# Second linear layer of a Winograd MLP with its matmul operands exchanged: tokens loaded as weights, weight columns streamed

## The chip, the cores and the metric

The kernel runs on one core of a Trainium2 chip. TensorE multiplies: it loads one operand (up to 128 x 128) and streams columns of the other past it into PSUM, which has eight banks of 128 x 512 floats. VectorE, ScalarE and GpSimd work element by element, SyncE issues most of the transfers, and 16 DMA engines carry them out. The metric is the device time of one execution in microseconds. Three runs of the kernel before took 874.29, 878.18 and 880.20 us.

## What is computed

Attention in which the heads are mixed before and after the softmax, then two linear layers with a SiLU between them:

```python
scores = einsum('bhij,hg->bgij', scale * q @ k.T, w_pre)      # 4 x 12 heads x 448 x 448
attn   = einsum('bhij,hg->bgij', softmax(scores), w_post)
x      = (attn @ v) laid out as 1792 tokens x 768
h      = x @ w_in                                             # w_in 768 x 2048
g      = h * (1 / (1 + exp(-h)))
out    = g @ w_out                                            # w_out 2048 x 768, float32
```

The change touches the last line alone.

## The kernel before

The first 440 us are attention. Both linear layers then use one level of a Winograd scheme with seven products: the tokens fall into two halves (u = 0, 1 count blocks of 448 tokens in a half), the inner dimension and the outer dimension into two halves each, and each product (k or m, 0 to 6) multiplies a sum or difference of token blocks by a sum or difference of weight blocks. The weight combinations are made on the fly from float64 input by `convert` (L38 to L100) during attention and the first layer and stored in DRAM (`wi_dram`, `wo_dram`), and come back through SyncE's queue as parts `wl` (L602).

Float32 accuracy is kept by halves: an operand x is cast to a rounded `high` part on ScalarE (`wh`, L607; `halve`, L626), and the rest is a subtraction (GpSimd for weights, L608; VectorE for tokens, L628). A product is then three matmuls per block: high x high, high x low, low x high.

The second layer of before has steps ("o", m, u, a), with a one of the three blocks of 128 output features (HC = 3) and HF = 8 blocks of the inner dimension. `product` (L611) makes one step: 24 matmuls, weights of 128 x 128 loaded and 448 token columns streamed, into one PSUM bank `ph`; four banks rotate. So the result has features on partitions. `evacuate` (L791) adds the products up on VectorE and ScalarE: U, V and the results. `put_out` (L835) turns each of the 24 results of 128 features x 448 tokens by four TensorE transposes into `ptt` (L842), copies them with the scale by ScalarE (L843) and stores them in rows of 128 features (L844).

The order of everything is written out by hand: a loop over the steps (L849) emits for each step its product, then the casts of weights due (`high_at`), the loads due (`load_at`), the transposes and stores of a finished result, the evacuation of the step before, and the pieces of `begin[s]`, where `put_at` (L638) has spread the token halves for the next product and the Winograd differences (`subtract`, L632). Engines wait for each other by semaphores alone, so each engine's own order is what this loop has emitted for it.

Of the kernel before, what the change touches and what calls it, by code (L numbers as in the profile page):

```python
# [103 lines left out]
def talking_heads_then_silu_mlp(  # L104
# [348 lines left out]
    jobs += [(wo_src[:, c, f], wo_dram[:, c * HF + f]) for c in range(HC) for f in range(HF)]  # L453
# [118 lines left out]
    box, gr = {}, {}  # L572
# [3 lines left out]
    steps = [(kind, k, u, a) for kind, n in (("i", HF), ("o", HC)) for k in range(7) for u in range(NU) for a in range(n)]  # L576
    step_of = {x: s for s, x in enumerate(steps)}
    NP = HF * HC // 4
    parts = [(src, ORDER[k], p) for src in (wi_dram, wo_dram) for k in range(7) for p in range(NP)]

    def part_of(kind, k, n):
        return ((kind == "o") * 7 + k) * NP + n // 4
# [3 lines left out]
    load_at, high_at = [[] for _ in steps], [[] for _ in steps]  # L586
    for j in range(WB, len(parts)):
        kind, m = ("i", "o")[j // (7 * NP)], j // NP % 7
        kind0, m0, p0 = ("i", "o")[(j - WB) // (7 * NP)], (j - WB) // NP % 7, (j - WB) % NP
        n = HC if kind0 == "i" else HF  # L590
        s = step_of[kind0, m0, NU - 1, (4 * p0 + 3) // n] + 1
        s = max(s, step_of[kind, m, 0, 0] - (10 if kind == "i" or m == 0 else 3))
        load_at[s].append(j)
        high_at[s + (2 if s < step_of["o", 0, 0, 0] - 2 else 1)].append(j)

    def load_part(j):
        src, k, p = parts[j]
        if src is wo_dram:
            for _ in conv:
                pass  # L600
        raws[j] = box["w"].tile([128, 4, 128], F32R, name="wl", tag="wl", bufs=WB)
        nc.sync.dma_start(out=raw(raws[j]), in_=src[:, 4 * p:4 * p + 4, k])  # L602

    def ready_part(j):
        wl = raws.pop(j)
        wh = box["w"].tile([128, 4, 128], F32R, name="wh", tag="wh", bufs=WB)
        nc.scalar.copy(out=wh, in_=raw(wl))  # L607
        nc.gpsimd.tensor_sub(out=wl, in0=raw(wl), in1=raw(wh))  # L608
        ready[j] = wh, wl

    def product(s, p):  # L611

        kind, k, u, a = steps[s]
        nk = HC if kind == "i" else HF
# [9 lines left out]
    def halve(src, dst):  # L624

        nc.scalar.copy(out=dst[:, 0], in_=src)  # L626
        yield
        nc.vector.tensor_sub(out=dst[:, 1], in0=src, in1=raw(dst[:, 0]))  # L628
# [16 lines left out]
    for kind, n, nk, blocks in (("i", HF, HC, xs), ("o", HC, HF, gr)):  # L645
        for m in range(7):
            for u in range(NU):
                s = step_of[kind, m, u, 0]
                todo = [lambda b=blocks, c=c, u=u, at=SOURCE[m]: halve(b[u][(*at, c)], ops[u][c]) for c in range(nk)]
                if m or u:  # L650
                    put_at(s - n, n - (kind == "i"), todo)
                elif kind == "o":
                    put_at(s - HF, HF - 1, todo)
        for d, (x, y, z) in enumerate(DIFFER):
            for u in range(NU):
                s = step_of[kind, d, u, 0] if kind == "o" or d > 1 else step_of[kind, 0, u, 0]
                put_at(s, n - 1 if kind == "i" else n, [
                    lambda b=blocks, c=c, u=u, x=x, y=y, z=z: subtract(
                        nc.vector, b[u][(*x, c)], b[u][(*y, c)], b[u][(*z, c)]) for c in range(nk)])
# [116 lines left out]
    ops[1] = [pair(gw, f"op1{c}") for c in range(HC)]  # L776
    for u in range(NU):
        gr[u] = {}
        for i, l in ((0, 1), (0, 0), (1, 1), (1, 0)):
            for f in range(HF):  # L780
                if (i, l) == (1, 0) and f < HC:
                    gr[u][i, l, f] = xs[u][0, 1, f]
                else:
                    gr[u][i, l, f] = gw.tile([128, T], F32, name=f"g{u}{i}{l}{f}")
    ps_t = pool("ps_tt", 3, space=PSUM)
    outs, sums, spare = [], [], []
# [4 lines left out]
    def evacuate(s, p):  # L791

        kind, k, u, a = steps[s]
        p = p[:, :T]
        if kind == "i":
            U, V = gr[u][1, 1, a], gr[u][0, 1, a]
        else:
            U, V = xs[u][0, 0, a], vp[a][:, u]
        M = firsts[:, a] if (kind, u) == ("i", 0) and k in (1, 3) and a < len(phs) else U

        def target(i, l):
            if kind == "i":
                return gr[u][i, l, a]
            return box["o"].tile([128, T], F32, name="oT", tag="oT", bufs=2)

        def finish(t, i, l, sign):
            if kind == "i":
                silu(t, sign)
            else:
                outs.append(lambda: put_out(2 * u + l, HC * i + a, t, sign))  # L810

        if k == 0:
            nc.scalar.copy(out=U, in_=p)
        elif k == 1:
            t = target(0, 0)
            nc.vector.tensor_add(out=t, in0=p, in1=M)
            finish(t, 0, 0, -1.0)
# [7 lines left out]
        elif k == 5:  # L825
            t = target(1, 0)
            nc.vector.tensor_sub(out=t, in0=U, in1=p)
            finish(t, 1, 0, 1.0)
        else:
            for (i, l), x in (((1, 1), U), ((0, 1), V)):  # L830
                t = target(i, l)
                nc.vector.tensor_add(out=t, in0=p, in1=x)  # L832
                finish(t, i, l, 1.0)

    def put_out(b, c, oT, sign):  # L835
        pt = ps_t.tile([128, 512], F32, name="ptt", tag="ptt")
        if spare:
# [56 lines left out]
    while outs:  # L894
        outs.pop(0)()
# [29 lines left out]
```

## Time and profile before

| | us |
|---|---|
| median of three runs (lowest, highest) | 878.18 (874.29, 880.20) |
| the profiled execution: time, span | 879.6, 877.9 |
| TensorE, VectorE, ScalarE, GpSimd busy in the span | 832.4, 625.6, 526.6, 406.7 |
| mean granted TensorE clock | 0.976 of full speed |

The span runs from the first to the last instruction of the program. PE is the matmul part of TensorE and PEld its weight loads, which overlap with matmuls; DVE is VectorE, ACT ScalarE, POOL GpSimd, SP SyncE. A matmul's shown duration reaches to the end of its pipeline, so successive ones overlap; the time from one to the next is read from counts in a stretch. The first layer lies at about 436 to 653 us, the second at 653 to 869, and what follows is the end of the last results.

### The profile page before, as it was taken

Reading aid. Unit: us, or ns where it says so; the run is one execution under the profiler, and the core shown is the slowest. Engines: PE = TensorE matmul, PEld = TensorE weight load, DVE = VectorE, ACT = ScalarE, POOL = GpSimd, SP = SyncE. Lnnn points to the kernel's source line nnn. Section 1 sums busy time; section 2 is a strip of 40 time slices with the busy share of each in tenths; the row PEclk is TensorE's granted clock in tenths of the full one; section 3 lists DMA queues with packets and bytes.
Section 4 is the critical chain, followed back from the end, with each engine's and each line's share of the span. In section 5 each row is a group of like instructions: output and inputs, shape, how many; then the busy total and the mean of one; then the engine's idle time right before and its main releaser. Section 6 shows DMA issues by size and latency. Waiting matters only on the chain.

```text
span 877.9 us, 27521 instructions
## 1 busy us (share of the span) xinstructions
PE 832.4 (95%) x11076; PEld 661.0 (75%) x11076; DVE 625.6 (71%) x1218; ACT 526.6 (60%) x1178; POOL 406.7 (46%) x679
## 2 busy tenths in 40 slices
PE   7998999899997999799899999999999999999997
PEld 5455676566665666466699999988899989999886
DVE  5554776477865877475788899999987689984332
ACT  4676887578875887587756653325694345343242
POOL 6131545353553645274877577556741233133020
PEclk8899999799998999899999999999999999999999
DMA  8668778787788777674625543455331142112224
GB/s 168 189 171 206 204 196 231 203 223 207 221 229 221 214 203 213 167 231 153 182 100 182 161 152 114 120 152 163 95 94 49 35 114 67 40 49 72 80 77 105
DMA packets 163655, 132.89 MB, mean 151 GB/s; under 512 B 51811, under 2 KB 157263, under 8 KB 163527
## 3 DMA queue, kind: packets, MB, share of 16 engines
q1 hardware_dynamic: 161299, 129.48, 52.8%
q8 instruction: 87, 1.43, 0.7%
q10 hardware_dynamic: 1812, 0.99, 0.5%
q0 software_dynamic: 416, 0.66, 0.3%
q14 instruction: 41, 0.34, 0.1%
HBM read 64.01 MB, written 27.53 MB: 104 GB/s over the span
## 4 chain that ended last, share of the span: by engine, by line
PE 74%; DVE 9%; DMA 5%; ACT 5%; issue 3%; POOL 2%; SPq 1%; ACTq 1%; POOLq 0%; DVEq 0%
PE ph L622 40%; PE pa L437 9%; PE po L368 8%; PE pp L399 7%; PE pqk L339 7%; DMA g<-st 3%; ACT e L409 1%; DVE nm L405 1%; DVE g L822 1%; ACT at L446 1%; DVE cg L92 1%; PE ptt L842 1%; DVE op L628 1%; PE pt L269 1%; PE pt L310 1%
## 5 line engine op out<-in xcount | busy, mean ns | idle before, releaser
L622 PE MATMUL ph<-op,wh 128*128 128x448 f32 x924 | 222.8, 369 | 2.7 <-DVE g L832 1.8
L608 POOL TENSOR_TENSOR wl<-wl,wh 128x512 fp32r<-128x512 f32 x84 | 122.6, 1475 | 153.6 <-ACT wh L607 150.2
L622 PEld LDWEIGHTS ph<-op,wh 128*128 128x128 f32 x924 | 172.4, 189 | 18.9 <-DVE g L832 2.1
L405 DVE TENSOR_REDUCE nm<-pp 128x1 f32<-128x448 f32 x184 | 106.0, 618 | 81.5 <-PE pp L399 81.1
L425 POOL TENSOR_SCALAR wr<-wpost,r 128x60 f32<-128x60 f32 x184 | 72.5, 407 | 185.0 <-DVE r L422 127.9
L409 ACT ACTIVATE e<-pp,nm 128x448 f32<-128x448 f32 x184 | 115.4, 631 | 45.4 <-DVE nm L405 42.7
L437 PEld LDWEIGHTS pa<-wr,e 64*64 64x64 f32 (+1 forms) x5888 | 98.4, 133 | 45.4 <-issue 27.4
L437 PE MATMUL pa<-wr,e 64*64 64x60 f32 (+1 forms) x5888 | 110.5, 221 | 14.4 <-ACT at L446 7.3
L622 PE MATMUL ph<-op,wl 128*128 128x448 f32 x462 | 119.5, 367 | 0.0
L66 POOL TENSOR_TENSOR cg<-cw,cg 128x256 f32<-128x256 f32 x96 | 75.6, 787 | 74.0 <-DVE cw L63 70.8
L399 PE MATMUL pp<-g,wpre 64*64 64x448 f32 x736 | 102.8, 578 | 6.4 <-ACT e L409 3.4
L368 PE MATMUL po<-at,v 120*64 120x120 f32 (+1 forms) x1536 | 88.8, 269 | 6.5 <-issue 4.9
L622 PEld LDWEIGHTS ph<-op,wl 128*128 128x128 f32 x462 | 87.1, 189 | 7.5 <-POOL wl L608 0.5
L446 ACT COPY at<-pa 120x960 f32<-120x960 f32 x92 | 89.9, 977 | 4.8 <-PE pa L437 4.8
L368 PEld LDWEIGHTS po<-at,v 120*64 120x64 f32 x1536 | 78.2, 140 | 19.3 <-issue 11.2
L607 ACT CAST wh<-wl 128x512 fp32r<-128x512 f32 x84 | 51.0, 617 | 53.4 <-DMA wl<-wo_dram 26.9
L344 DVE COPY st<-pqk 120x448 f32<-120x448 f32 (+1 forms) x89 | 54.8, 617 | 33.0 <-PE pqk L339 18.1
L90 ACT ACTIVATE cg<-cg,ebias 128x256 int32<-128x256 int32 x96 | 49.5, 516 | 39.2 <-DVE cg L86 37.8
L92 DVE SCALAR_TENSOR_TENSOR cg<-cw,cg 128x256 int32<-128x256 int32 x96 | 56.0, 583 | 17.9 <-ACT cg L90 17.5
L622 PE MATMUL ph<-x,wh 128*128 128x448 f32 x252 | 64.9, 366 | 0.0
L339 PEld LDWEIGHTS pqk<-kh,qh 64*120 64x120 f32 (+1 forms) x186 | 18.9, 176 | 45.8 <-issue 15.9
L346 ACT COPY st<-pqk 120x448 f32<-120x448 f32 (+1 forms) x89 | 48.0, 539 | 6.6 <-DMA g<-st 3.4
(120 smaller groups left out, 1381.1 us busy)
## 6 DMA issues: line engine op xcount, KB each, us to landing
g<-st SPq DMA_DIRECT2D x132, 210.0 KB
cw<-in_moe_w_in SPq DMA_DIRECT2D x48, 256.0 KB
cw<-in_moe_w_out SPq DMA_DIRECT2D x48, 256.0 KB
wi_dram<-cg SPq DMA_DIRECT2D x24, 448.0 KB
wo_dram<-cg SPq DMA_DIRECT2D x24, 448.0 KB
wl<-wi_dram SPq DMA_DIRECT2D x42, 256.0 KB
wl<-wo_dram SPq DMA_DIRECT2D x42, 256.0 KB
g<-st SPq DMA_DIRECT2D x48, 175.0 KB
```

The source lines that it names most:

```text
L66: nc.gpsimd.tensor_mul(out=e, in0=m, in1=e)
L92: nc.vector.scalar_tensor_tensor(out=e, in0=hi, scalar=-2 ** 31, in1=e, op0=ALU.bitwise_and, op1=ALU.bitwise_or)
L339: nc.tensor.matmul(ps[i][:m, :S], lhsT=q_[rows, hh, :m], rhs=k_[rows], start=(step == 0), stop=(step == 2))
L368: nc.tensor.matmul(po[i * D:(i + 1) * D, c * m:(c + 1) * m], lhsT=vs[b, h][:, i, j, :], rhs=ats[n][:, j, h + i, :m], start=(j == 0), stop= ...
L399: nc.tensor.matmul((self, other)[r].p[HP * c:HP * (c + 1), :S], lhsT=wpre[rows], rhs=gs[self.n][rows, o // R + c * np + p, :], start=True, ...
L405: nc.vector.tensor_reduce(out=self.nm, in_=self.p[:GP, :S], axis=AX.X, op=ALU.max, negate=True)
L409: nc.scalar.activation(out=self.e, in_=self.p[:GP, :S], func=AF.Exp, bias=self.nm, scale=1.0, accum_out=sums)
L425: nc.gpsimd.tensor_scalar(out=g.wr, in0=wpost.rearrange("p g i -> p (g i)"), scalar1=r[:, i:i + 1], scalar2=1.0, op0=ALU.mult, op1=ALU.mult)
L437: nc.tensor.matmul(half[64 * c:64 * c + m, s, j * GH:(j + 1) * GH], lhsT=g.e[rows, j * JT + c * JH:j * JT + c * JH + m], rhs=g.wr[rows], s ...
L446: nc.scalar.copy(out=ats[self.n].rearrange("p j g t -> p (j g) t")[:, :, o:o + 2 * R].rearrange("p x (c i) -> p x c i", i=RH), in_=pa[:KV] ...
L608: nc.gpsimd.tensor_sub(out=wl, in0=raw(wl), in1=raw(wh))
L622: nc.tensor.matmul(p[:, :T], lhsT=w, rhs=x, start=(n == 0), stop=(n == len(todo) - 1))
```

## The change

In the second layer the operands change places. For a block c of 128 tokens (seven blocks in 896 tokens, over both u) the halves of the tokens are loaded as the 128 x 128 operand, and the weights of one inner block f, now 384 features wide, are streamed. A step is ("o", k, g, c): group g holds the two inner blocks f = 2g and 2g + 1, so it has six matmuls. All seven c go through group 0, then all through group 1, and so on; the seven sums of a product stay open in seven PSUM banks (four `ph`, three `pt`) until group 3. A result is then 128 tokens x 384 features, tokens on partitions, and is stored as it is.

Token tiles of the second layer are now one tile of 2 x 448 for both u, so a cast, a subtraction or a difference covers 896 columns. `outer[f]` holds the two halves of f. The half of f for product m + 1 is made when group f // 2 of product m is through. Weight parts have three blocks of 128 (one f) in place of four, 56 parts in place of 42; a load is emitted ten steps ahead of its group at the latest, and its cast four steps later. The scale moves from the copy of the results into the evacuation, a SCALAR_TENSOR_TENSOR in place of an addition. In the diff, the pieces that choose tiles for the same data are left out.

```diff
-    steps = [(kind, k, u, a) for kind, n in (("i", HF), ("o", HC)) for k in range(7) for u in range(NU) for a in range(n)]
+    NT2, W2, FG = NU * T // 128, HC * 128, HF // 2
+    steps = [("i", k, u, a) for k in range(7) for u in range(NU) for a in range(HF)]
+    steps += [("o", k, g, c) for k in range(7) for g in range(FG) for c in range(NT2)]
...
+    parts += [(wo_dram, ORDER[k], slice(HC * f, HC * f + HC)) for k in range(7) for f in range(HF)]
...
     for j in range(WB, len(parts)):
...
-        s = max(s, step_of[kind, m, 0, 0] - (10 if kind == "i" or m == 0 else 3))
+        s = max(used(j - WB)[1] + 1, used(j)[0] - 10)
         load_at[s].append(j)
-        high_at[s + (2 if s < step_of["o", 0, 0, 0] - 2 else 1)].append(j)
+        high_at[s + (2 if s < step_of["o", 0, 0, 0] - 2 else 4)].append(j)
...
+    def product_out(s, p):
+
+        _, k, g, c = steps[s]
+        todo = []
+        for f in range(2 * g, 2 * g + 2):
+            wh, wl = (x.rearrange("p c w -> p (c w)") for x in ready[part_of("o", k, f)])
+            xh, xl = (x.rearrange("p u t -> p (u t)")[:, c * 128:(c + 1) * 128] for x in outer[f])
+            todo += [(0, xh, wh), (1, xl, wh), (2, xh, wl)]
+        todo.sort(key=lambda t: t[0])
+        for n, (_, x, w) in enumerate(todo):
+            nc.tensor.matmul(
+                p[:, :W2], lhsT=x, rhs=w, start=(g == 0 and n == 0), stop=(g == FG - 1 and n == len(todo) - 1))
...
+    outer, o0 = [], step_of["o", 0, 0, 0]
+    for f in range(HF):
+        for m in range(7):
+            if m:
+                s = step_of["o", m - 1, f // 2, 0] + NT2 + 3 * (f % 2)
+            else:
+                s = o0 - 7 + 3 * f if f < 2 else o0 + NT2 * (f // 2 - 1) + 3 * (f % 2)
+            begin[s].append(lambda f=f, at=SOURCE[m]: halve(gp[(*at, f)], outer[f]))
         for d, (x, y, z) in enumerate(DIFFER):
+            begin[step_of["o", d, f // 2, 2 + 3 * (f % 2)]].append(
+                lambda f=f, x=x, y=y, z=z: subtract(nc.vector, gp[(*x, f)], gp[(*y, f)], gp[(*z, f)]))
...
-    def put_out(b, c, oT, sign):
-        pt = ps_t.tile([128, 512], F32, name="ptt", tag="ptt")
...
-        for j in range(NJ):
-            nc.tensor.transpose(pt[:JT, j * 128:(j + 1) * 128], oT[:, j * JT:(j + 1) * JT], ident)
-        nc.scalar.mul(ob, pt[:JT].rearrange("p (j c) -> p j c", j=NJ), sign * 2.0 ** -WEXP)
-        nc.sync.dma_start(out=out[b * T:(b + 1) * T, c * 128:(c + 1) * 128].rearrange("(j p) c -> p j c", p=JT), in_=ob)
+    def evacuate_out(k, c, p):
+
+        U, V = us[c], vs2[c]
+
+        def add(out, sign, to):
+            nc.vector.scalar_tensor_tensor(
+                out=out, in0=p, scalar=sign * 2.0 ** -WEXP, in1=to, op0=ALU.mult, op1=ALU.add)
+
+        if k in (0, 2):
+            nc.scalar.mul((U, V)[k // 2], p, -2.0 ** -WEXP)
+        elif k in (1, 5):
+            t = box["o"].tile([128, W2], F32, name="oT", tag="oT", bufs=4)
+            add(t, -1.0, U)
+            put_out(c, k // 5, 0, t)
+        elif k == 3:
+            add(U, 1.0, U)
+            sums.append(lambda: nc.vector.tensor_add(out=V, in0=V, in1=U))
+        elif k == 4:
+            add(U, -1.0, U)
         else:
+            for i, x, queue in ((1, U, nc.sync), (0, V, nc.scalar if c == NT2 - 1 else nc.sync)):
+                add(x, 1.0, x)
+                put_out(c, i, 1, x, queue)
+
+    def put_out(c, i, l, t, queue=nc.sync):
+
+        n = c * 128
+        while n < (c + 1) * 128:
+            u = n // T
+            end = min((c + 1) * 128, (u + 1) * T)
+            row = (2 * u + l) * T + n - u * T
+            queue.dma_start(out=out[row:row + end - n, i * W2:(i + 1) * W2], in_=t[n - c * 128:end - c * 128])
+            n = end
```

How TensorE's order moves, in the second layer. Before, at the end of a step of the second product: names are output<-operands, with `op`, `x`, `xr` and `firsts` the tiles of the token halves of f = 0 to 7.

```order
L622 MATMUL ph<-x_10787,wl 128x448
L622 MATMUL ph<-xr_10782,wl 128x448
L622 MATMUL ph<-xr_10783,wl 128x448
L842 MATMUL ptt<-ident,oT 112x128 x4
L622 MATMUL ph<-op_8845,wh 128x448
L622 MATMUL ph<-op_8846,wh 128x448
```

After, group 0 of the first product from the last `ph` bank (c = 3) to the first `pt` bank (c = 4): `op_8364` and `op_8365` are the halves of f = 0, `op_8366` and `x_10756` those of f = 1.

```order
L629 MATMUL ph<-wh,op_8364 128x384
L629 MATMUL ph<-wh,op_8366 128x384
L629 MATMUL ph<-wh,op_8365 128x384
L629 MATMUL ph<-wh,x_10756 128x384
L629 MATMUL ph<-wl,op_8364 128x384
L629 MATMUL ph<-wl,op_8366 128x384
L629 MATMUL pt<-wh,op_8364 128x384
L629 MATMUL pt<-wh,op_8366 128x384
```

Six matmuls of 384 columns go to a bank before the next one's turn, and no transpose stands anywhere in the layer.

ScalarE's order at the start of the layer. Before, from the last SiLU pieces (L789) to the first product's second token block:

```order
L789 ACTIVATE g_8900<-g_8900 128x448
L789 ACTIVATE g_8884<-g_8884 128x448
L626 CAST op_8845<-g_8885 128x448
L626 CAST op_8846<-g_8886 128x448
L626 CAST op_8847<-g_8887 128x448
L607 CAST wh<-wl 128x512
L813 COPY x_118<-ph 128x448
```

After, the same place:

```order
L816 ACTIVATE g_8871<-g_8871 128x448
L816 ACTIVATE g_8855<-g_8855 128x448
L650 CAST x_10757<-g_8858 128x896
L615 CAST wh<-wl 128x384
L650 CAST xr_10753<-g_8859 128x896
L650 CAST op_8364<-x_121 128x896
L650 CAST x_10759<-g_8860 128x896
L615 CAST wh<-wl 128x384 x2
```

The casts of f = 2 and 3 now stand behind the last SiLU, and the second product's cast of f = 0 (into `op_8364`) stands ahead of the first product's cast of f = 4 (into `x_10759`).

SyncE's queue at the end of the program. Before:

```order
L602 DMA wl<-wo_dram 128x4x128 x2
L844 DMA out<-ob 112x4x128 x6
L844 DMA out<-x_12632 112x4x128
L844 DMA out<-x_12640 112x4x128
L844 DMA out<-x_12677 112x4x128
L844 DMA out<-op_12685 112x4x128
```

After:

```order
L610 DMA wl<-wo_dram 128x3x128 x4
L880 DMA out<-x_118 128x384
L880 DMA out<-v_10899 128x384
L880 DMA out<-x_118 128x384
L880 DMA out<-v_10899 128x384
L880 DMA out<-x_119 128x384
L880 DMA out<-v_10899 128x384
L880 DMA out<-x_119 64x384 x2
```

The stores of the last product follow the last weight load in one row, two for each block c (four for c = 3, which crosses from u = 0 to u = 1; the very last stands on ScalarE's queue).

## Rows read from the trace of the kernel before

**Rows 1.** The page: span, busy time and slices of TensorE, its clock, the chain by line.

```profile
span 877.9 us, 27521 instructions
...
PE 832.4 (95%) x11076; PEld 661.0 (75%) x11076; DVE 625.6 (71%) x1218; ACT 526.6 (60%) x1178; POOL 406.7 (46%) x679
...
PE   7998999899997999799899999999999999999997
...
PEclk8899999799998999899999999999999999999999
...
PE ph L622 40%; PE pa L437 9%; PE po L368 8%; PE pp L399 7%; PE pqk L339 7%; DMA g<-st 3%; ACT e L409 1%; DVE nm L405 1%; DVE g L822 1%; ACT at L446 1%; DVE cg L92 1%; PE ptt L842 1%; DVE op L628 1%; PE pt L269 1%; PE pt L310 1%
```

**Rows 2.** Busy time by stretch: warm-up, second layer, tail, its third product.

```profile
core 0: us, PE busy (x) PEld busy (x) DVE busy (x) ACT busy (x) POOL busy (x), PEclk, DMA share, GB/s
7.90:8.70 0.80, 0.80 (x10) 0.80 (x9) 0.58 (x2) 0.53 (x1) 0.80 (x1) 1.00 1.33 161
652.70:868.70 216.00, 215.49 (x1081) 195.87 (x1080) 139.70 (x209) 89.07 (x176) 56.15 (x39) 1.00 0.24 65
868.70:877.90 9.20, 3.41 (x26) 2.40 (x23) 2.31 (x4) 3.34 (x6) 0.00 (x0) 0.97 0.57 151
713.30:744.70 31.40, 30.91 (x155) 27.76 (x154) 29.56 (x40) 17.18 (x34) 11.29 (x9) 1.00 0.26 73
```

**Rows 3.** Timeline, start and end of the second layer and the last stores (SPq).

```profile
start us, us, engine line op out<-in xcount [idle before <-releaser]
...
652.70 0.77 PE L622 MATMUL ph<-op,wh 128*128 128x448 f32 x3
...
864.29 6.06 SPq L844 DMA_DIRECT2D out<-x  x3
...
868.56 0.37 PE L622 MATMUL ph<-xr,wl 128*128 128x448 f32 x1
...
872.93 0.91 SPq L844 DMA_DIRECT2D out<-ob  x2
```

**Rows 4.** Chain of waits, in order of time (start, us, what), in the second layer.

```profile
725.04 0.44 PE ptt L842 x4
725.48 92.42 PE ph L622 x456
...
868.93 0.45 PE ptt L842 x4
```

**Rows 5.** Groups by line and shape, second layer, TensorE.

```profile
line engine op names shapes xcount | busy us, mean ns | idle before us <-releasers
...
L622 PE MATMUL ph<-x,wh 128*128 128x448 f32 x252 | 64.9, 366 | 0.0
...
L622 PEld LDWEIGHTS ph<-x,wh 128*128 128x128 f32 x252 | 47.3, 188 | 3.9
...
L842 PE MATMUL ptt<-ident,oT 128*112 128x128 f32 x72 | 10.3, 272 | 0.0
```

**Rows 6.** Timeline, warm-up matmuls of line 516 at the program's start.

```profile
7.80 0.97 PEld L516 LDWEIGHTS pa<-ident 128*128 128x128 f32 x8
...
7.89 1.07 PE L516 MATMUL pa<-ident 128*128 128x128 f32 x8
```

**Rows 7.** Groups by line and shape, second layer, other engines.

```profile
L632 DVE TENSOR_TENSOR g<-g,g 128x448 f32<-128x448 f32 x58 | 47.2, 843 | 0.0
...
L607 ACT CAST wh<-wl 128x512 fp32r<-128x512 f32 x38 | 23.0, 621 | 27.7 <-DMA wl<-wo_dram 26.9 <-PE ph L622 0.5
...
L626 ACT CAST op<-g 128x448 fp32r<-128x448 f32 x27 | 13.4, 564 | 7.2 <-PE ph L622 7.2
...
L827 DVE TENSOR_TENSOR oT<-x,ph 128x448 f32<-128x448 f32 x6 | 3.7, 616 | 5.2 <-PE ph L622 5.2
```

**Rows 8.** Waits in the second layer (total us, times, longest), engines, then SyncE's queue.

```profile
engine line waited for: us in total, times, longest us
...
ACT wh L607 <- DMA wl<-wo_dram: 26.9, 22, 5.5
...
SPq L602 <- PE ph L622: 97.1, 25, 18.3
```

**Rows 9.** DMA engines from 869.9 to 877.9 us, in 40 slices of 0.2 us.

```profile
DMA  0000089999999999999999999999996200000000
GB/s 0 0 0 0 15 207 215 218 241 259 248 236 282 310 320 243 274 294 254 287 271 279 292 271 289 256 279 259 282 277 187 77 3 0 0 0 0 0 0 0
DMA packets 2785, 1.38 MB, mean 173 GB/s; under 512 B 96, under 2 KB 2784, under 8 KB 2784
```

More of the change, by code (lines that the diff above doesn't have):

```diff
@@ L624, in halve @@
     def halve(src, dst):
-        nc.scalar.copy(out=dst[:, 0], in_=src)
+        hi, lo = (dst[:, 0], dst[:, 1]) if not isinstance(dst, tuple) else dst
+        nc.scalar.copy(out=hi, in_=src)
         yield
-        nc.vector.tensor_sub(out=dst[:, 1], in0=src, in1=raw(dst[:, 0]))
+        nc.vector.tensor_sub(out=lo, in0=src, in1=raw(hi))
     def subtract(eng, out, a, b):
@@ L776, in talking_heads_then_silu_mlp @@
     ops[1] = [pair(gw, f"op1{c}") for c in range(HC)]
+    for i, l in ((0, 1), (0, 0), (1, 1), (1, 0)):
+        for f in range(HF):
+            gp[i, l, f] = xt[0, 1, f] if (i, l) == (1, 0) and f < HC else pair(gw, f"g{i}{l}{f}", F32)
     for u in range(NU):
[L778 to L784, printed above, removed]
+        gr[u] = {at: x[:, u] for at, x in gp.items()}
     ps_t = pool("ps_tt", 3, space=PSUM)
-    outs, sums, spare = [], [], []
+    sums = []
     def silu(t, sign):
@@ L793, in evacuate @@
         kind, k, u, a = steps[s]
+        if kind == "o":
+            return evacuate_out(k, a, p[:, :W2])
         p = p[:, :T]
[L795 to L810, printed above, removed]
+        U, V = gr[u][1, 1, a], gr[u][0, 1, a]
+        M = firsts[:, a] if u == 0 and k in (1, 3) and a < len(phs) else U
         if k == 0:
@@ L855, in talking_heads_then_silu_mlp @@
             xr = [pair(xr_p, f"xr{c}") for c in range(3)]
+            x10, x11 = ([pair(x_p, f"x1{l}{c}") for c in range(HC)] for l in range(2))
+            halves = ops[0] + x10 + xr[:2] + x11 + [pair(gw, "firsts"), xr[2]] + ops[1]
+            outer += [(halves[2 * f], halves[2 * f + 1]) for f in range(HF)]
         if (kind, m, u, a) == ("o", 0, 0, 0):
             box["o"] = pool("oo", 1)
[L858 to L865 removed]
+            v7 = box["o"].tile([128, NT2, W2], F32, name="v7")
+            vs2 = [v7[:, c] for c in range(NT2)]
+            us = [xt[0, 0, c // 2][:, c % 2, :W2] for c in range(NT2 - 1)]
+            us.append(box["o"].tile([128, W2], F32, name="u6"))
+        p = None
+        if kind == "o":
+            if u == 0:
+                accs[a] = bank(ps_h, "ph") if a < 4 else ps_t.tile([128, 512], F32, name="pt", tag="pt")
+            p = accs[a]
+            product(s, p)
+        elif s >= len(phs):
             p = bank(ps_h, "ph")
@@ L889, in talking_heads_then_silu_mlp @@
                     active.remove(x)
+            if not last or not active:
+                break
         if kind == "i":
```

98 lines of the change are left out of this document (39 added, 59 removed).

## The prediction

> **What bounds the kernel now.** I read the page first [rows 1]: TensorE is busy 95% of a span of 877.9 us, the granted clock is at its upper level (2.4 GHz) for nearly all of it, and the chain that ended last runs through the matmul line L622 for 40% of the span, its largest part. The change touches only the second linear layer, so the next view was the busy time by stretch [rows 2]. From the first to the last matmul of that layer TensorE is busy 215.49 of 216.00 us, VectorE 139.70, ScalarE 89.07, GpSimd 56.15, the DMA engines 24%. The layer is bound by TensorE, and an edit there is worth what it does to TensorE's instruction stream and to the tail behind the last matmul.
>
> The layer starts at 652.70 and its last matmul starts at 868.56 [rows 3]: 215.9 us. The chain of waits prices one matmul: 456 in 92.42 us, 202.7 ns each [rows 4]. So 1008 matmuls are 204.3 us. Between them stand groups of four transposes, 0.44 us each [rows 4]; 72 transposes, so 18 groups, lie before the last product matmul [rows 5]: 7.9 us. The remaining 3.7 us are short gaps. Behind the last matmul come 877.9 - 868.6 = 9.3 us of tail.
>
> **The change, part by part.**
>
> *Product matmuls.* Seven products x 4 groups x 7 token blocks x 6 is 1176 matmuls of 384 columns in place of 1008 of 448; the columns are the same, 451,584. What counts is the time of one. At 2.4 GHz 448 columns are 186.7 ns, and the row shows 202.7, so 16.0 ns lie on top. If that grows with the columns, 384 cost 173.7 ns; if it is fixed per matmul, 160.0 + 16.0 = 176.0. I take 175, between the two, since the trace has no other width of this type at the same weight shape: 205.8 us, 1.5 more than now (bounds -0.0 and +2.7).
>
> Could the weight load set the pace instead? A load of 128x128 is shown with 188 ns [rows 5], and each begins as the matmul before it begins, so the layer alone doesn't tell. The warm-up matmuls at the start do: eight loads of the same 128x128 shape end to end take 0.97 us, with 0.19 for a single one, which makes (0.97 - 0.19) / 7 = 111 ns from one to the next, at the same granted clock [rows 2, 6]. A load that can be repeated every 111 ns is hidden under 174 ns of columns.
>
> *Transposes.* All 96 go, with their 24 ScalarE copies. The 18 groups ahead of the last product matmul give back 7.9 us of TensorE; the other six belong to the tail.
>
> *Operand halves and differences.* Now 56 casts, 56 subtractions and 32 differences of 896 columns instead of twice as many of 448. From 564 ns at 448 and 621 at 512 a ScalarE cast costs 0.9 ns per column [rows 7], so 0.97 us at 896 and 0.50 at 384. VectorE takes 616 ns for 448 columns when undisturbed [rows 7]; at 1.04 to 1.07 ns per column that is 1.1 us at 896 and 0.55 at 384. In a product of 168 x 175 ns = 29.4 us VectorE then has at most 16 x 1.1 + 7 x 0.55 = 21.5 us, plus what GpSimd's concurrent subtractions add: the 843 ns mean of L632 against 616 undisturbed [rows 7] is 0.23 per instruction, so some 4 us. That fits under 29.4; cover is TensorE, and without it 25 us of VectorE would be the bound. From the second product on, an operand's half is written three groups, 22 us, ahead of its use. Only in the first product is it tight: ScalarE meets the second product's cast of f = 0, which waits for TensorE to finish group 0, ahead of the first product's cast of f = 4. From that moment two casts (1.9 us), two weight casts (1.0) and two casts (1.9) reach f = 5 at 4.9 us, and VectorE's chain of five 1.1 us instructions ends at about 7 to 8. Group 2 starts 42 x 175 ns = 7.35 us after group 0's end and reads that half half a microsecond later. I charge 2 us for gaps in the whole layer, between 0 and 5, near what stands there now (3.7).
>
> *Weights.* 56 loads of 192 KB for 42 of 256 KB, in six buffers as before. SyncE's queue waits for TensorE to free a buffer (97.1 us in total), and ScalarE waited 26.9 us in all for such a load in the stage without a cost to TensorE [rows 8]. A buffer is now freed three groups before its use; loads, casts and GpSimd's subtractions hide behind these 22 us. I cost them at nothing; without that cover a load is about 3 to 4 us late.
>
> *Accumulators.* Seven banks stay open for 29.4 us. A bank is read one step after its last matmul and written again six steps, 6.3 us, after that. VectorE's reading (0.55 us) or ScalarE's hides there unless VectorE is more than five microseconds behind.
>
> *Tail.* Now the last product's results leave through transposes and copies, and the last store is issued at 872.93 to 873.84 [rows 3]; the DMA engines are busy from 870.8 to 876.3 [rows 9], and 1.5 us later the program ends. With the change the results of the last product all finish in the last group of 7.35 us: 14 blocks, 2.75 MB. After the last matmul start there are 0.37 us for that matmul [rows 5], two VectorE additions (1.1) with a backlog of 0.3, then issue and first data (0.9: a store issued at 870.0 moves from 870.8 on [rows 3, 9]), 0.5 of data and 1.5 to the end: 4.7 us, and I add 0.1 for the queue, 4.8, if issuing sets it. Were the data to move at no more than the present tail's mean of 1.38 MB in 5.5 us, 250 GB/s, 2.75 MB would take 11.0 us from 4.5 us before the last matmul, and the end would be at 6.5 + 1.5 = 8.0 us. The present rows are of 512 bytes and the new of 1536, so I take 5.5, nearer to the first; 9.3 - 5.5 = 3.8 us are saved.
>
> **The sum.** 652.70 + 1175 x 0.175 + 2.0 = 860.3 for the last matmul, against 868.56: -8.3 us. With the tail -3.8: -12.1 us. The profiled execution took 879.6 us, 1.4 above the median of 878.18, so against the median I forecast 866 us. The lower end of this case is 173.7 ns, no gaps and 4.8 us of tail (-16.3, 862); the upper one 176.0 ns, 5 us of gaps and 8.0 of tail (-5.4, 873).
>
> **Rivals.**
>
> *The load sets the pace.* If a matmul can't follow the one before it sooner than now, because its 128-column load must finish first (188 ns shown, then 14 to spare), 1176 matmuls cost 202.7 each: 238.4 us, 34.1 more. The sum is then 652.7 + 238.2 + 5.5 = 896.4, 18.5 slower than the span: 897 us, with the gaps hidden. For it: loads are busy 195.87 of 216.00 us [rows 2], and each ends just ahead of its matmul. Against it: the 111 ns of [rows 6]. The point that decides is 185 ns per matmul: above it 1176 of them eat what the transposes and the tail return. Chance 0.08. The Trainium skill, page "Perfetto Trace Analysis", section "Identifying the Most-Contended Engine", says that TensorE's headroom is to be read from its arithmetic and from the share of time in weight loads and not from matmul busy time. By that rule a stage at 91% of load time has no room for 168 more loads, and it speaks against the change; here the trace bears it out only in that the busy shares agree, since a shown load is longer than the time from load to load in the warm-up.
>
> *Operands late.* If VectorE's subtractions meet GpSimd as often as in the busiest present product, 29.56 busy of 31.40 us [rows 2], TensorE waits about 3 us at each of the three later groups of the first product, or at the boundaries behind products 1 and 3, whose seven additions come on top: 9 us in place of 2, so -12.1 + 7 = -5 us, 873. For it speaks that 7 to 8 us meet a deadline of 7.9; against it that only the first product is so tight. Chance 0.14.
>
> *The 16 ns vanish.* If they belong to the present pairing of widths, 384 columns cost 160.0 ns: 652.7 + 188.0 + 2 + 5.5 = 848.2, 849 us against the median. Nothing but the clock speaks for it. Chance 0.04. The Trainium skill, page "TensorE: Matmul & The Clock Gate", section "Back-to-back issue gap", has the columns over the clock plus 2.5 ns. By it, 448 columns would be 189 ns where the row shows 202.7, so the rows decide; at 384 it would give 162.5 and a layer of 191 us.
>
> That the change doesn't do what it says I leave out: the order of instructions shows the 1176 matmuls, no transposes and the new stores.
>
> **Chances and range.** The forecast has 0.74. Within 1% (8.8 us, about what a measurement of this kernel can tell) lie the operands' case and the dear end of the forecast, some 0.20 in all; slower by more than 1% is the load's case and a rest, 0.10; faster 0.70. The range 859 to 874 holds the forecast's own ends, the operands' case and a little for the spread of the runs; it leaves out the load's case above and the vanished 16 ns below.
>
> **What would show it.** The new matmul line, in the chain, at 174 to 176 ns each; a group of 42 in 7.35 us. Loads of 128x128 still shown at about 190 ns or less. No idle time of TensorE above 1 us except in the first product's groups 2 and 3, put down to VectorE or ScalarE. The end about 5.5 us behind the last matmul, the DMA engines busy to 1.5 us before it. The prediction is wrong if the matmuls stand at 185 ns or more, if gaps sum to over 5 us, or if the stores still run 7 us after the last matmul.

## The result, and the profile after

The change makes the kernel faster: 862.22 us in the median of six runs (857.05 to 865.42) against 876.23 of the kernel before in the same comparison (872.95 to 880.20). The ratio is 0.9852, with a 95% interval of 0.9821 to 0.9883, so 14.0 us in the medians. The profiled execution took 857.05 us with a span of 855.3. One run of an experiment below, the halves one group ahead, took 976 us at a granted clock of 0.751 and is counted nowhere.

The page of the profile after, with the lines that answer to [rows 1]:

```profile
span 855.3 us, 27555 instructions
...
PE 811.6 (95%) x11148; PEld 661.6 (77%) x11148; DVE 625.6 (73%) x1137; ACT 511.0 (60%) x1114; POOL 428.5 (50%) x693
...
PE   7898999799998999999899999999999999999997
...
PEclk9899999899999999999999999999999999999999
...
PE 71%; DVE 12%; DMA 6%; ACT 4%; issue 3%; POOL 2%; SPq 1%; ACTq 1%; DVEq 0%; POOLq 0%
```

The span is 22.6 us shorter than in [rows 1], which is more than the medians say. The trace shows why: the second layer starts at 644.64 here and at 652.70 in [rows 3], though of the work ahead of it the change moves only the first operand halves and weights of this layer. In the eight profiles of the experiments below the start lies anywhere from 639.4 to 652.4, with the order of before as with the new one. So the start of the layer is scatter, and only two stretches can be compared between profiles: from the first product matmul's start to the last one's (the layer), and from there to the end (the tail).

The busy time by stretch answers to [rows 2]: layer, tail, and the third product.

```profile
core 0: us, PE busy (x) PEld busy (x) DVE busy (x) ACT busy (x) POOL busy (x), PEclk, DMA share, GB/s
644.60:848.90 204.30, 204.22 (x1177) 203.67 (x1176) 142.89 (x135) 78.39 (x124) 80.23 (x54) 1.00 0.23 70
848.90:855.30 6.40, 0.33 (x2) 0.01 (x1) 1.37 (x3) 0.00 (x0) 0.00 (x0) 0.76 0.65 217
703.40:732.50 29.10, 29.10 (x170) 29.10 (x169) 24.49 (x20) 13.43 (x22) 13.80 (x8) 1.00 0.32 96
```

The layer is still TensorE's: busy for 204.22 of 204.30 us at a granted clock of 1.00 (2.4 GHz). VectorE has 24.49 of 29.10 us in the third product, where it had 29.56 of 31.40 before. From first to last matmul start the layer takes 848.89 - 644.64 = 204.25 us, 11.6 fewer than the 215.86 of [rows 3]. The tail is 855.32 - 848.89 = 6.43 us, 2.9 fewer than 9.32. Together that is -14.5 us, and the medians say -14.0.

The chain of waits answers to [rows 4] (start, us, what):

```profile
678.67 3.12 PE pt L629 x18
...
681.79 4.16 PE ph L629 x24
```

The first row is the three `pt` banks of one group, the second the four `ph` banks of the next: 7.28 us for 42 matmuls, 173.3 ns each, and nothing between them. From the first matmul of a bank to that of the next, over the whole layer, the median is 173.3 ns per matmul as well.

The timeline answers to [rows 3]: the layer's start, its longest gap, and the end.

```profile
644.64 0.69 PE L629 MATMUL ph<-wh,op 128*128 128x384 f32 x3
...
666.34 1.08 DVE L652 TENSOR_TENSOR op<-g,op 128x896 fp32r<-128x896 f32 x1
...
667.47 0.19 PEld L629 LDWEIGHTS ph<-wh,op 128*128 128x128 f32 x1 [0.40 <-DVE op L652]
...
846.15 0.37 SPq L880 DMA_DIRECT2D out<-v  x1
...
846.73 1.11 SPq L880 DMA_DIRECT2D out<-x  x2
...
847.18 0.56 DVE L854 SCALAR_TENSOR_TENSOR x<-pt,x 128x384 f32<-128x384 f32 x1
...
847.93 1.20 SPq L880 DMA_DIRECT2D out<-v  x2
...
848.89 0.34 PE L629 MATMUL pt<-wl,op 128*128 128x384 f32 x1
...
849.23 0.54 SPq L880 DMA_DIRECT2D out<-x  x1
849.27 0.56 DVE L854 SCALAR_TENSOR_TENSOR u<-pt,u 128x384 f32<-128x384 f32 x1
...
851.36 0.55 SPq L880 DMA_DIRECT2D out<-u  x1
```

At 667.47 TensorE has waited 0.40 us for VectorE's subtraction, which ended at 667.42. It made the low half of f = 7, read by the fourth matmul of group 3 of the first product. A shorter stop of this kind stands at 659.81, in group 2; there is no other in the layer. At the end a store takes SyncE 0.33 to 0.37 us up to 846.15 and leaves as soon as its data are ready. Then block c = 3, which crosses from u = 0 to u = 1, goes out in four stores of 64 rows, and these hold the queue from 846.73 to 849.13, 0.6 us each, where a whole one took 0.33 to 0.37. The `x` of c = 4 is ready at 847.74 and leaves at 849.23. That delay of 1.5 us stays to the end: the last `u` is ready at 849.83 and leaves at 851.36.

Groups by line and shape in the second layer and tail, answering to [rows 5, 7] (columns as there):

```profile
L616 POOL TENSOR_TENSOR wl<-wl,wh 128x384 fp32r<-128x384 f32 x54 | 80.9, 1517 | 109.0 <-ACT wh L615 105.3 <-PE ph L629 3.7
L629 PE MATMUL ph<-wh,x 128*128 128x384 f32 x168 | 47.1, 334 | 0.0
L656 DVE TENSOR_TENSOR g<-g,g 128x896 f32<-128x896 f32 x29 | 41.9, 1446 | 0.0
...
L629 PEld LDWEIGHTS ph<-wh,x 128*128 128x128 f32 x168 | 30.8, 188 | 0.0
...
L615 ACT CAST wh<-wl 128x384 fp32r<-128x384 f32 x53 | 24.9, 511 | 7.1 <-DMA wl<-wo_dram 6.9
```

A load is still shown with 188 ns, now longer than the 173.3 ns in which one matmul follows another. ScalarE's wait for weights, 26.9 us in [rows 8], is 6.9 here.

DMA engines from 841 to 855.3 us in 40 slices, answering to [rows 9]:

```profile
DMA  0000000002999999997748494899999999900000
GB/s 0 0 0 0 0 0 0 0 0 95 382 361 361 374 365 361 378 361 262 180 112 185 116 206 112 198 352 365 370 365 382 353 365 370 352 17 0 0 0 0
DMA packets 2048, 2.75 MB, mean 193 GB/s; under 512 B 256, under 2 KB 2048, under 8 KB 2048
```

The stores run at 350 to 380 GB/s at the start and at the end, where the rows of [rows 9] ran at 250; in the middle, 847.4 to 850.3, at 110 to 260, which is about the stretch of the four half stores, though the engines are busy for 40 to 90% of it. They end at 853.6, some 1.7 us ahead of the end of the program.

### The profile page after: what moved, and what is told of

It reads as the page before. It is cut to its first block, busy times and chain, and to the rows that moved or that the text cites. A ratio compares the mean times of both kernels' runs of the same rounds, so it can differ in the third digit from the quotient of the medians.

```text
span 855.3 us, 27555 instructions
## 1 busy us (share of the span) xinstructions
PE 811.6 (95%) x11148; PEld 661.6 (77%) x11148; DVE 625.6 (73%) x1137; ACT 511.0 (60%) x1114; POOL 428.5 (50%) x693
## 4 chain that ended last, share of the span: by engine, by line
PE 71%; DVE 12%; DMA 6%; ACT 4%; issue 3%; POOL 2%; SPq 1%; ACTq 1%; DVEq 0%; POOLq 0%
PE ph L645 17%; PE ph L629 12%; PE pt L629 9%; PE pa L437 9%; PE po L368 7%; PE pp L399 7%; PE pqk L339 7%; DMA g<-st 3%; DVE op L652 2%; ACT e L409 1%; DVE nm L405 1%; DVE g L836 1%; DVE cg L92 1%; ACT at L446 1%; DVE g L838 1%
## 5 line engine op out<-in xcount | busy, mean ns | idle before, releaser
L616 POOL TENSOR_TENSOR wl<-wl,wh 128x384 fp32r<-128x384 f32 (+1 forms) x98 | 144.1, 1487 | 124.7 <-ACT wh L615 119.7
L645 PE MATMUL ph<-op,wh 128*128 128x448 f32 x672 | 155.6, 367 | 2.7 <-DVE g L846 1.8
L645 PEld LDWEIGHTS ph<-op,wh 128*128 128x128 f32 x672 | 125.3, 188 | 15.6 <-DVE g L846 2.1
L437 PEld LDWEIGHTS pa<-wr,e 64*64 64x64 f32 (+1 forms) x5888 | 96.4, 131 | 47.4 <-issue 29.2
L437 PE MATMUL pa<-wr,e 64*64 64x60 f32 (+1 forms) x5888 | 108.5, 218 | 16.7 <-ACT at L446 7.4
L645 PE MATMUL ph<-op,wl 128*128 128x448 f32 x336 | 86.6, 366 | 0.0
L615 ACT CAST wh<-wl 128x384 fp32r<-128x384 f32 (+1 forms) x98 | 52.1, 556 | 33.1 <-DMA wl<-wi_dram 26.1
L645 PEld LDWEIGHTS ph<-op,wl 128*128 128x128 f32 x336 | 63.0, 188 | 5.5 <-POOL wl L616 0.5
L399 PEld LDWEIGHTS pp<-g,wpre 64*64 64x64 f32 x736 | 23.2, 133 | 33.2 <-ACT e L409 14.5
```

Of the source, the lines that this page charges most:

```text
L399: nc.tensor.matmul((self, other)[r].p[HP * c:HP * (c + 1), :S], lhsT=wpre[rows], rhs=gs[self.n][rows, o // R + c * np + p, :], start=True, ...
L437: nc.tensor.matmul(half[64 * c:64 * c + m, s, j * GH:(j + 1) * GH], lhsT=g.e[rows, j * JT + c * JH:j * JT + c * JH + m], rhs=g.wr[rows], s ...
L645: nc.tensor.matmul(p[:, :T], lhsT=w, rhs=x, start=(n == 0), stop=(n == len(todo) - 1))
```

## Experiments

In each, layer and tail are read as above. "Before" is 215.86 and 9.32, "after" is 204.25 and 6.43.

### One width after another

The seven products of the changed kernel get different numbers of streamed columns; everything else stays.

```diff
+            wide = W2 if g == 0 and n == 0 else (384, 320, 256, 192, 128, 64, 384)[k]
-                p[:, :W2], lhsT=x, rhs=w, start=...
+                p[:, :wide], lhsT=x, rhs=w[:, :wide], start=...
```

> Left out: parts of the sums of products 1 to 5, since all but the first matmul of each bank stream only 320, 256, 192, 128 and 64 columns (products 0 and 6 keep 384). Read from the starts of successive matmuls inside a step. Theory A (time grows with the columns, 173.4 ns at 384, so 0.4516 ns each, down to the time from load to load): 145 ns at 320, 116 at 256, about 111 at 192, 128 and 64. Theory B (16 ns fixed on top of the columns at 2.4 GHz; it would give 176 at 384, where the changed kernel showed 173.4, so it starts behind): 149 at 320, 123 at 256, 111 below. Theory C (the shown load of 188 ns sets a pace): no less than 173 at any width.

One run took 864.14 us. Time per matmul, as the median over the banks: 173.3 ns at 384 columns, 146.7 at 320, 120.0 at 256, and 112 at 192. Busy time in products 1, 3, 4, 5 and 6:

```profile
682.00:706.00 24.00, 24.00 (x165) 24.00 (x164) 21.81 (x17) 10.72 (x17) 12.87 (x8) 1.00 0.21 66
...
729.00:751.00 22.00, 19.39 (x166) 18.88 (x165) 22.00 (x15) 13.84 (x24) 14.48 (x10) 1.00 0.28 81
752.00:789.00 37.00, 36.05 (x168) 35.72 (x167) 25.91 (x31) 7.82 (x12) 9.64 (x8) 0.52 0.11 33
790.00:825.60 35.60, 35.60 (x166) 35.60 (x165) 12.47 (x14) 9.60 (x16) 12.71 (x8) 0.50 0.22 67
825.70:856.00 30.30, 30.30 (x169) 30.27 (x169) 8.71 (x15) 4.66 (x8) 7.25 (x6) 0.96 0.29 92
```

And the chain there, in product 1 (320 columns), product 4 (128) and product 5 (64):

```profile
688.19 3.52 PE ph L630 x24
...
767.60 3.84 PE pt L630 x18
...
816.93 5.12 PE ph L630 x24
```

From 384 to 320 to 256 columns the step falls by 26.7 ns each time, and 64 columns at 2.4 GHz are 26.7. So the columns cost what the clock says, and a fixed 13.3 ns lie on top (173.3 - 160.0, 146.7 - 133.3, 120.0 - 106.7). Growth in proportion to the columns would have given 145 and 116. At 192 columns, 80 + 13.3 = 93 is not reached: the step stops at 112 ns, close to the 111 from load to load in [rows 6]. So there the load does seem to set the pace; at 384 columns that is some 61 ns away. In products 4 and 5 the granted clock is half, 1.2 GHz, and the step is 213 ns for 128 and for 64 columns alike (3.84 / 18 and 5.12 / 24), so it isn't the columns that set it; it is about twice the 112. The total is no measure here, as VectorE became the bound in products 2 and 3 (busy 22.00 of 22.00 us in the latter) and the clock in 4 and 5.

The first matmuls of product 6 still run at 1.2 GHz, and there 384 columns take 320 ns, the columns alone:

```profile
826.81 0.52 PE L630 MATMUL ph<-wh,x 128*128 128x384 f32 x1
...
827.13 0.84 PE L630 MATMUL ph<-wl,op 128*128 128x384 f32 x2
```

What lies on top of the columns was there at the full clock only.

The form "fixed per matmul" of the forecast is thus right at the full clock and for 256 to 384 columns, with 13.3 ns in place of 16. For 448 columns 13.3 gives 200.0, and [rows 4] show 202.7: there the steps go round in a row of 207, 203, 202, 203 and 199 ns, and why is not shown.

### The kernel before without its transposes

The loop order and operands are those of before; the transposes are gone, and ScalarE copies the result with features on partitions, in two pieces, 512 columns as before, for the same stores.

```diff
-        pt = ps_t.tile([128, 512], F32, name="ptt", tag="ptt")
...
-        for j in range(NJ):
-            nc.tensor.transpose(pt[:JT, j * 128:(j + 1) * 128], oT[:, j * JT:(j + 1) * JT], ident)
-        nc.scalar.mul(ob, pt[:JT].rearrange("p (j c) -> p j c", j=NJ), sign * 2.0 ** -WEXP)
+        flat = ob.rearrange("p j c -> p (j c)")
+        nc.scalar.mul(flat[:, :384], oT[:JT, :384], sign * 2.0 ** -WEXP)
+        nc.scalar.mul(flat[:, 384:], oT[:JT, 320:], sign * 2.0 ** -WEXP)
```

> The kernel before without its 96 transposes: ScalarE scales the untransposed result into the tile that is stored, in two pieces, so the stored values aren't the reference's. Theory A (the transposes stand on TensorE's path): the second layer from first to last matmul 215.9 - 7.9 = 208.0 us, its gaps of about 3.7 us still there, the tail 1 to 2 us shorter, 9 to 10 us in all. Theory B (the transposes fill time in which TensorE would wait for VectorE anyway, so the gain came from elsewhere): the layer at 212 us or more, under 5 us in all.

Median of four runs 860.06 us, ratio 0.9804 [0.9734, 0.9874]. Layer 204.09, tail 6.44. The chain from 690 to 800 us is one piece, and the layer by stretch:

```profile
689.84 110.25 PE ph L622 x544
```

```profile
639.40:843.50 204.10, 204.10 (x1008) 189.17 (x1008) 137.51 (x212) 96.12 (x204) 57.04 (x40) 1.00 0.26 74
```

110.25 us for 544 matmuls are 202.7 ns each, with no gap anywhere in the layer. The expectation was 208.0: the 7.9 us of transposes would go and the gaps would stay. The gaps went as well. Taking the transposes off the old order therefore gives -11.8 us in the layer and -2.9 in the tail, which is the whole effect of the change (-11.6 and -2.9). The exchange of operands by itself neither gains nor costs (204.09 us of layer in the old order, 204.25 in the new); what it does is make results that need no transposes.

### Transposes kept, but not read

To see whether the gaps came from TensorE's transposes themselves or from whoever waits for them, they stay in TensorE's order, and only ScalarE's copy reads past them.

```diff
         for j in range(NJ):
             nc.tensor.transpose(pt[:JT, j * 128:(j + 1) * 128], oT[:, j * JT:(j + 1) * JT], ident)
-        nc.scalar.mul(ob, pt[:JT].rearrange("p (j c) -> p j c", j=NJ), sign * 2.0 ** -WEXP)
+        flat = ob.rearrange("p j c -> p (j c)")
+        nc.scalar.mul(flat[:, :384], oT[:JT, :384], sign * 2.0 ** -WEXP)
+        nc.scalar.mul(flat[:, 384:], oT[:JT, 320:], sign * 2.0 ** -WEXP)
```

> The kernel before with its 96 transposes in place, but ScalarE scales the untransposed result, so no engine reads what they write (the stored values aren't the reference's). Without any transposes the layer took 204.1 us and had no gap; with them 215.9, of which 7.9 are the transposes and 3.9 more are gaps. Theory A (the gaps come from ScalarE: it stands in its queue until the transposes are through, and the next product's casts behind it come late): the layer at 212 us, no idle time in front of matmuls that read token halves. Theory B (they come from TensorE itself, where transposes and matmuls change over, or from VectorE's results being late for the transposes): the layer stays at 215 to 216 us. Tail under both: 6.4 to 8 us, since the stores no longer wait for TensorE.

One run took 874.94 us. Layer 212.81, tail 8.56. TensorE waits for nobody in the layer; what is left above the matmuls (204.1) is the transposes and 0.8 us of changing over. So 215.86 - 212.81 = 3.05 us of the gaps are ScalarE's standing in its queue. The timeline of the kernel before shows one such place:

```profile
713.01 0.60 PE L842 MATMUL ptt<-ident,oT 128*112 128x128 f32 x4
...
713.70 0.60 ACT L843 ACTIVATE ob<-ptt 112x512 f32<-112x512 f32 x1 [2.36 <-issue]
714.19 1.02 ACT L626 CAST xr<-g 128x448 fp32r<-128x448 f32 x2
...
714.80 0.19 PEld L622 LDWEIGHTS ph<-xr,wh 128*128 128x128 f32 x1 [0.34 <-ACT xr L626]
```

And the same place with the transposes unread:

```profile
706.97 1.02 ACT L626 CAST xr<-g 128x448 fp32r<-128x448 f32 x2
...
707.10 0.60 PE L842 MATMUL ptt<-ident,oT 128*112 128x128 f32 x4
```

Before, ScalarE has idled 2.36 us ahead of a copy that can only run behind the transposes; behind the copy stand two casts of token halves, and TensorE's next loads wait for these. The profile puts that idle time down to "issue"; that it is the wait for the transposes is what the second fence shows, where the same casts run just ahead of the transposes and no load waits. An order on ScalarE, and not the transposes' own time, made these gaps. The tail of 8.56 lies above the 6.4 to 8 that was expected:

```profile
865.56 0.62 DVE L832 TENSOR_TENSOR oT<-ph,x 128x448 f32<-128x448 f32 x1 [4.57 <-PE ptt L842]
```

VectorE's last additions write into two buffers `oT`, and wait for the transposes behind the last product matmul, which still read them.

### Halves one group ahead

The changed kernel makes each half of a later product about three groups ahead. Here it is seven steps ahead (one group, 7.3 us) for the first f of a group and four (4.2 us) for the second.

```diff
-                s = step_of["o", m - 1, f // 2, 0] + NT2 + 3 * (f % 2)
+                s = step_of["o", m, f // 2, 0] - (NT2 - 3 * (f % 2))
```

> The changed kernel with the token halves of products 1 to 6 made seven and four steps ahead of their group (7.3 and 4.2 us) in place of three groups ahead (22 us). Theory A (the 22 us lead is what removed TensorE's gaps; VectorE meets differences and GpSimd and comes late): gaps of 0.5 us or more at a dozen or more group starts, 5 to 15 us in all. Theory B (any lead of a group hides it, since cast and subtraction together are 0.94 + 1.1 to 1.9 us): the layer within 1 us of 204.3.

Median of three runs 857.94 us, ratio 0.9796 [0.9744, 0.9848]. Layer 203.67, tail 6.43, and the two stops of the changed kernel are gone too:

```profile
643.30:847.10 203.80, 203.80 (x1178) 203.76 (x1176) 139.19 (x135) 79.72 (x124) 76.25 (x54) 1.00 0.24 71
```

The long lead of the change isn't what removed the gaps, and it made those two stops: it is what put the second product's cast ahead of the first product's.

### Halves three steps ahead

```diff
-                s = step_of["o", m - 1, f // 2, 0] + NT2 + 3 * (f % 2)
+                s = step_of["o", m, f // 2, 0] - (3 - f % 2)
```

> The changed kernel with the halves of products 1 to 6 made three and two steps (3.1 and 2.1 us) ahead of their group. One group ahead cost nothing (203.7 us for the layer). Theory A (VectorE has slack enough that only its own latency counts: casts of 0.94 us, subtractions of 1.1 us, 1.9 when GpSimd is met): 24 groups with up to 0.5 us each, the layer at 204 to 212 us. Theory B (VectorE's queue is near its limit in products 0 to 3, so anything late piles up): 1 to 2 us at each group of products 1 to 3, the layer at 215 us or more.

One run took 869.46 us. Layer 211.91, tail 6.44. Six gaps, each in group 0 of a product from the second on: one matmul starts 1.23, 2.47, 1.23, 1.85, 0.85 and 0.85 us after the one before it, 8.1 us in all above the usual step with the slower one behind each. The longest, at the start of the third product:

```profile
708.42 1.08 DVE L656 TENSOR_TENSOR g<-g,g 128x896 f32<-128x896 f32 x1
...
709.42 0.55 DVE L854 SCALAR_TENSOR_TENSOR oT<-pt,x 128x384 f32<-128x384 f32 x1
...
709.89 1.70 DVE L652 TENSOR_TENSOR x<-g,op 128x896 fp32r<-128x896 f32 x1
...
711.64 0.45 PE L629 MATMUL ph<-wh,x 128*128 128x384 f32 x1 [2.13 <-DVE x L652]
```

The subtraction that TensorE waits for starts as soon as VectorE is through with a difference and an evacuation ahead of it. So late operands cost about what that rival said (its 9 us of gaps) once the lead is some three steps, 3.1 us. They cost it at the six product starts, where the evacuations of the product before stand in the way too (VectorE's, or ScalarE's behind products 0 and 2), and not at all the groups.

### Stores on two queues

In the changed kernel only the very last store is issued from ScalarE's queue. Here the second result of every block is.

```diff
-            for i, x, queue in ((1, U, nc.sync), (0, V, nc.scalar if c == NT2 - 1 else nc.sync)):
+            for i, x, queue in ((1, U, nc.sync), (0, V, nc.scalar)):
```

> The changed kernel with the last product's second result of each token block stored through ScalarE's queue, so SyncE issues 8 of the 16 last stores. Theory A (SyncE's issuing sets the tail: its last store was issued 1.5 us after its data was ready): the last store is issued at most 0.4 us after VectorE's last addition and the tail from the last matmul's start is 4.9 us in place of 6.4. Theory B (the data rate sets it: 2.75 MB at 365 GB/s from the first data on): the DMA engines are busy without a break and the tail stays over 6 us. In the run's time 1.5 us is less than the runs scatter; the profile decides.

Median 863.30 us, ratio 0.9838 [0.9782, 0.9893]. Layer 204.22, tail 5.87: between the two expectations.

```profile
856.98 0.56 DVE L854 SCALAR_TENSOR_TENSOR u<-pt,u 128x384 f32<-128x384 f32 x1
...
857.56 0.33 SPq L880 DMA_DIRECT2D out<-u  x1
```

```profile
DMA  0000000699999999967698979999999999200000
GB/s 0 0 0 0 0 0 0 251 369 354 379 359 359 383 359 359 383 221 182 133 216 226 280 177 280 398 388 369 388 379 378 388 384 364 103 0 0 0 0 0
```

The last `u` now leaves 0.02 us after it is ready (857.54), 0.96 us after the last matmul's start in place of 2.47. That is 1.5 us earlier, but the end comes only 0.56 us earlier: the DMA engines now run at 364 to 398 GB/s to the last data. The queue was the first limit, the data is the second. The dip in the middle is there with two queues as well (133 to 280 GB/s), so the half stores' data moves slowly too, and not only their issuing: splitting a block costs on both sides.

### The last product spread out

The halves one group ahead, the stores on two queues, and the last product's groups 2 and 3 block by block: a block is finished every 12 matmuls, 2.1 us, where before all seven finish in the last 7.3 us.

```diff
-    steps += [("o", k, g, c) for k in range(7) for g in range(FG) for c in range(NT2)]
+    steps += [("o", k, g, c) for k in range(6) for g in range(FG) for c in range(NT2)]
+    steps += [("o", 6, g, c) for g in range(2) for c in range(NT2)]
+    steps += [("o", 6, g, c) for c in range(NT2) for g in (2, 3)]
-                s = step_of["o", m - 1, f // 2, 0] + NT2 + 3 * (f % 2)
+                s = step_of["o", m, f // 2, 0] - (NT2 - 3 * (f % 2))
-            for i, x, queue in ((1, U, nc.sync), (0, V, nc.scalar if c == NT2 - 1 else nc.sync)):
+            for i, x, queue in ((1, U, nc.sync), (0, V, nc.scalar)):
```

> The changed kernel with three edits together: halves one group ahead, the second results on ScalarE's queue, and in the last product groups 2 and 3 taken block by block, so that a block is finished every 12 matmuls (2.1 us) in place of every 6. Theory A (the tail is the time of 2.75 MB of stores that begin too late, at 365 to 380 GB/s or at SyncE's issuing): the tail is 4.4 to 4.8 us in place of 6.4, the layer 203.7, 2 us less than the changed kernel in all. Theory B (the tail is the latency of the last store alone: addition, issue, data, confirmation): it stays at 5.8 or more, as with two queues alone.

Median of six runs 856.26 us, ratio 0.9770 [0.9716, 0.9823].

```profile
646.10:849.80 203.70, 203.70 (x1177) 203.69 (x1175) 139.91 (x135) 79.60 (x124) 77.34 (x54) 1.00 0.24 74
849.80:854.50 4.70, 0.34 (x2) 0.01 (x1) 1.02 (x2) 0.00 (x0) 0.00 (x0) 0.89 0.40 146
```

Layer 203.70, tail 4.69: 208.4 us against 210.7 of the changed kernel. With one block's two stores left behind the last matmul, the tail comes down to what the forecast had, 4.8 us, for the case in which issuing sets it.

### The changed kernel again, beside it

> The changed kernel unaltered, on the same chip as the others, so that the spread-out end is compared with it and not only with the kernel before. Both theories: 0.985 of the kernel before, the layer 204.2 us, the tail 6.4.

Median 858.67 us, ratio 0.9805 [0.9754, 0.9857]; layer 204.21, tail 6.45. The medians put the version above 2.4 us ahead of it, as the profiles do (2.3), but the two intervals overlap: the runs alone don't tell these two kernels apart.

This repeat also says how far the medians can be trusted. Here they put the change at 877.23 - 858.67 = 18.6 us, where the first comparison had 14.0; the profiles say 14.5 and 14.5. That the first one lies within 0.5 us of the profiles is luck.

## Why the prediction came out as it did

| term | forecast | measured |
|---|---|---|
| matmuls | +1.5 us (175 ns) | -0.5 (173.3 ns) |
| transposes in the layer | -7.9 | -7.9 |
| gaps | -1.7 (3.7 to 2.0) | -3.2 (3.6 to 0.4) |
| tail | -3.8 (to 5.5) | -2.9 (to 6.43) |
| sum | -12.1 | -14.5 in the profiles, -14.0 in the medians (-18.6 in the repeat) |

The terms count 1008 and 1176 matmuls, as the forecast does; from the first to the last start there is one step less. So the forecast's terms add up to -11.9 where its sum, by 1175 steps, has -12.1, and by the starts each gap figure is 0.2 us longer.

The forecast of 866 us was 4 us high, with the mechanism right: TensorE bounds the layer before and after, and what its instruction stream loses in transposes, the time loses.

**Product matmuls.** 1.7 ns too dear each, 2.0 us in all. The forecast split the difference between a cost that grows with the columns and one that is fixed; the widths show it fixed, at 13.3 ns. That its bound for the other form, 173.7, came nearest is chance. The 16.0 read from [rows 4] was the mean over uneven steps of 199 to 207 ns and didn't carry over to 384 columns. Both its bounds, 173.7 and 176.0, lie above what was measured.

**Load sets the pace.** Refuted twice. The changed kernel shows loads of 188 ns every 173.3 ns, so shown loads overlap one another; and the widths show a floor of 112 ns, where the forecast had read it from the warm-up [rows 6]. The shares of load time went from 91% to 99.7% (203.67 of 204.30 us) while the layer became 11.6 us shorter. The Trainium skill, page "Perfetto Trace Analysis", section "Identifying the Most-Contended Engine", judges TensorE's headroom by its arithmetic and by the share of time in weight loads. The second half of that does not hold for this trace.

**The 16 ns vanish.** No: 13.3 of them stay at the full clock. The Trainium skill, page "TensorE: Matmul & The Clock Gate", section "Back-to-back issue gap", gives the columns over the clock plus 2.5 ns, as the gap of a single isolated matmul and not of a stream with weight loads. An estimate by it is 162.5 ns at 384 columns; 173.3 were measured, and the measurement decides.

**Transposes.** -7.9 us, as worked out from [rows 4, 5]; left in but unread they cost 8.7 us of the layer (212.81 against 204.09).

**Gaps.** Here a step of the forecast failed, though in the cheap direction. It charged "2 us for gaps in the whole layer, between 0 and 5, near what stands there now (3.7)", and never asked what made the 3.7. The gaps of before belonged to the transposes: ScalarE stood at their copies with casts queued behind. The change removes these copies, so it removes the gaps with them, 3.05 us by the experiment, and this part belonged with the transposes in the sum. What remains stands in the first product: 0.2 us in group 2, whose deadline the forecast had worked out, and 0.4 us in group 3, which it had named only among the places to look.

**Operands late.** Not at a lead of a group or more; at three steps it is real, 8 us.

**Halves, differences and weights.** Hidden as forecast. VectorE was put at 25.5 us of a product at most, and the third product shows 24.49. The 896-column differences take 1446 ns in the mean where the forecast had 1.1 us plus 0.23 for GpSimd: less than TensorE's cover of 29.1 us by a good margin. GpSimd's own busy time rose from 56.15 to 80.23 us for the same number of weights, and nobody waited for it.

**Accumulators.** No wait for a bank in the layer, as forecast.

**Tail.** 0.9 us too short. The step that failed is "0.1 for the queue": the last store left 1.5 us after its data were ready, a delay that the timeline shows to begin at the four half stores of c = 3, which the forecast left out. With a second queue 0.56 us come back, and then the data sets the end: 2.75 MB at 350 to 400 GB/s, well above the 250 of the forecast's second end, but at 110 to 280 while the half stores run. How the delay divides between the issuing of the half stores and their data was not tried. The old kernel without transposes has the same tail (6.44) by another way, with stores of 512-byte rows, so taking the transposes off gains as much there too; that the two tails come out equal is chance.

## What to carry to other kernels

An instruction that leaves an engine takes with it the wait of whoever read its result: find in the timeline which engine stands at that reader, and what is queued behind it, and count that with the removed instruction. What bounds a change of operand order is the time from one matmul's start to the next, and the smallest such time in the same trace, not the shown length of a load. Where results all finish in the last group, count the stores per queue and their issue time (here the two halves of a split store cost more than two whole ones), and let the last product finish its blocks one by one.

## Of the hardware, unexpected

- Weight loads overlap one another: shown with 188 ns each, they follow at 173.3 ns in the changed kernel and at 112 ns with 192 streamed columns.
- In the experiment with the widths TensorE's clock was granted at half from 753.26 to 828.35 us, nearly all of the 128- and 64-column products, 36.05 busy of 37.00 us and 35.60 of 35.60. The fall came behind a stop of 2.95 us for VectorE at 748.8 us, within a shorter one from 752.4; the clock did not come back while short matmuls followed one another without a gap, and was back in the next product of 384 columns (0.96 in its mean). What of this is the stop and what the width was not tried apart.
- Stores whose rows have 1536 bytes ran at 350 to 400 GB/s, those of 512 bytes [rows 9] at 250 in the mean. Four stores of 64 rows each, also of 1536 bytes, moved 110 to 280 GB/s; with the last product spread out each took 0.47 to 0.60 us to issue, where one of 128 rows took 0.33 to 0.35.
